# Third pair of tiles loaded before the token weights, with the first batch's work reordered and some evictions and casts moved to ScalarE

## The chip, the cores and the metric

One NeuronCore of a Trainium2 chip. The metric is the device time of one execution in microseconds (us). The profiled span of an execution is about 1.8 us shorter than its time.

## The reference

Two stages. The first is a linear recurrence per head with a decay, on q, k, v of shape 4 x 8 x 768 x 64. The second is a Wave-MLP on its result x (4 x 768 x 512).

```python
state = gamma * state + k_t v_t^T          # per batch and head
y_t   = scale * q_t state                  # x: heads side by side, 512 wide
theta = x @ w_theta
y     = w_tok_r @ (x * cos(theta)) + w_tok_i @ (x * sin(theta))   # over the 768 tokens
u     = x + y
out   = u + maximum(u @ w_ch, 0)
```

## The kernel before

The 768 tokens of a batch are three *pairs* of 128-token tiles, so there are twelve pairs. Pairs 0, 1, 2 are batch 0, and pair 3 opens batch 1. For each pair k, q and v are loaded (0.52 MB each), cast or scaled to bf16 ("prep"), k and q are flipped on TensorE, and the recurrence (called retention below) is done blockwise: attention block `ret_A`, mask on VectorE, product `ret_Y`, state products `ret_S` and `ret_I`. Then x is flipped back (`x_pe`), theta is made, ScalarE takes sine and cosine, and VectorE makes z (`zmul`). The token mixing `moe_M(m, lo, hi)` of output tile m takes z of tiles lo to hi. The token weights come as twelve tiles ("wtok", w0 to w5, real and imaginary), are cast and flipped (`w_cast`, `w_flip`, `w_out`). A flip is a transpose on TensorE, and an eviction is the copy of a result out of its PSUM bank, which frees the bank.

All loads are issued by one queue in program order, through buffers that are reused in turn:

```python
def load_wtok(r, t0):
    t = io.tile([P, S], FT, name="wtok", bufs=4)
    nc.sync.dma_start(out=t, in_=src[t0 * P:(t0 + 1) * P, :])
...
loads("p0 th p1 w0 p2 w1 w2 p3 w3 ch p4 w4 p5 w5")

def w_cast(t0):
    for r in range(2):
        row = work.tile([P, S], BF, name="wrow", bufs=5)
        nc.gpsimd.tensor_copy(row, wdma[r, t0])     # frees the wtok buffer
```

All transposes and the output products share two PSUM banks, tag "tr":

```python
ps   = psum.tile([P, 2, NP, P], BF, name="kq_ps", tag="tr", bufs=2)  # flip of k or q
w_ps = psum.tile([P, nT, P],    BF, name="w_ps",  tag="tr", bufs=2)  # flip of token weights
u_ps, o_ps, x_ps                                                     # the same two banks
```

The end of pair 3's iteration (n = nG = 3), cut:

```python
moe_M(first, 0, 2)                  # first = output tile 2
ret_S(n, 0); state_out(n, 0); ret_A(n, 1); ret_mask(n, 1); ret_Y(n, 0)
moe_U(done)                         # flips u of tiles 0 and 1
prep(n + 1, "k", (AC,)); preps(DP)  # q4: half on VectorE, half on GpSimd
moe_M(first, 2, 4)
w_tok(3)                            # flips w3, real and imaginary
moe_M(first, 4, nT); moe_u(first)
for i, t in enumerate(done):        # tiles 0 and 1
    flip(n + 1, "kq"[i])            # k4, then q4
    moe_O(t); moe_out(t)
```

Of the kernel before, what the change touches and what calls it, by code (L numbers as in the profile page):

```python
# [14 lines left out]
FT = mybir.dt.float32  # L15
BF = mybir.dt.bfloat16
# [16 lines left out]
def kernel(  # L33
# [17 lines left out]
    nc = tc.nc  # L51
# [39 lines left out]

    def load_wtok(r, t0):
        src = (moe_w_tok_r, moe_w_tok_i)[r]
        t = io.tile([P, S], FT, name="wtok", bufs=4)
        nc.sync.dma_start(out=t, in_=src[t0 * P:(t0 + 1) * P, :])
        wdma[r, t0] = t

    def loads(order):
        for what in order.split():
            if what == "th":  # L100
                load_w512("th", moe_w_theta)
            elif what == "ch":
                load_w512("ch", moe_w_ch)
            elif what[0] == "w":
                for r in range(2):
                    load_wtok(r, int(what[1:]))
            else:
                for name in "kqv":
                    load(int(what[1:]), name)

    loads("p0 th p1 w0 p2 w1 w2 p3 w3 ch p4 w4 p5 w5")


    warm = const.tile([P, dm], BF)
# [72 lines left out]
            copy(t, ps)  # L187
        st[n, name + "T"], st[n, name + "_ps"] = t, ps

    def flip_out(n, name):  # L190
        nc.vector.tensor_copy(st[n, name + "T"], st[n, name + "_ps"])

    def flip_dma(n, name):
        t = work.tile([P, 2, NP, P], BF, name="kqT", bufs=6)
# [109 lines left out]
    def x_out(n, copy):  # L304
        b, g = divmod(n, nG)
        copy(xs[b][:, 2 * g:2 * g + 2, :],
             st[n, "x_ps"].rearrange("p a j e -> p a (j e)"))

    def theta(n, a):
        th_ps = psum.tile([P, dm], FT, name="th_ps", tag="acc", bufs=2)  # L310
        for j in range(NP):
            nc.tensor.matmul(th_ps, st[n, "xT"][:, a, j, :], wth[:, j, :], start=(j == 0),  # L312
                             stop=(j == NP - 1))
        cs = work.tile([P, 2, dm], BF, name="cs", bufs=3)
        nc.scalar.activation(cs[:, 0, :], th_ps, AF.Sin, bias=halfpi, scale=1.0)  # L315
        nc.scalar.activation(cs[:, 1, :], th_ps, AF.Sin, bias=zerob, scale=1.0)  # L316
        st[n, "cs", a] = cs
# [53 lines left out]

    def moe_out(m):
        b, t0 = divmod(m, nT)
        ot = work.tile([P, dm], FT, name="ot", bufs=8)
        nc.vector.scalar_tensor_tensor(ot, mo[m]["o"], 0.0, mo[m]["u"], ALU.max, ALU.add)  # L375
        mo[m]["ot"] = ot

# [3 lines left out]

    wrow = {}

    def w_cast(t0):
        for r in range(2):
            row = work.tile([P, S], BF, name="wrow", bufs=5)
            nc.gpsimd.tensor_copy(row, wdma[r, t0])  # L387
            wrow[r, t0] = row

    def w_flip(r, t0, copy=True):  # L390
# [12 lines left out]
    def w_tok(t0):  # L403
        for r in range(2):
            w_flip(r, t0)
# [56 lines left out]
    def keep_busy(times):  # L462
        for _ in range(times):
            nc.tensor.matmul(warm_ps, warm[:, 0:P], warm, start=True, stop=True)
# [35 lines left out]
    theta(0, 1)  # L500
    flip(1, "q")
    prep(1, "v", PP)
    w_cast(0)
    x_pe(0, None)
    ret_A(1, 0)
    ret_mask(1, 0)
    x_out(0, DV.tensor_copy)
    keep_busy(3)
    ret_S(1, 0)
    state_out(1, 0)  # L510
# [1 line left out]
    ret_mask(1, 1)  # L512
    ret_Y(1, 0)
    ret_I(1, 0)
    w_flip(0, 0)
    ret_S(1, 1)
    state_out(1, 1)
    ret_I(1, 1)
    ret_Y(1, 1)
    ret_out(1, 0, AC.copy)  # L520
    ret_out(1, 1, DV.tensor_copy)
    w_flip(1, 0)
    prep(2, "k", (PL,))
    zmul(0, 0)
    flip(2, "k")
    prep(2, "q", DP)
    theta(1, 0)
    zmul(0, 1)
    theta(1, 1)
    moe_M(0, 0, 1)  # L530
    flip(2, "q")
    prep(2, "v", PP)
    w_cast(1)
    w_cast(2)
    x_pe(1, AC.copy)
    moe_M(0, 1, 2)
    ret_A(2, 0)
    ret_mask(2, 0)
    ret_S(2, 0)
    state_out(2, 0)  # L540
    ret_A(2, 1)
    ret_mask(2, 1)
    zmul(1, 0)
    ret_Y(2, 0)
    ret_I(2, 0)
    ret_I(2, 1)
    w_flip(0, 1, False)
    w_flip(1, 1, False)
    ret_Y(2, 1)
    ret_out(2, 0, AC.copy)  # L550
    ret_out(2, 1, DV.tensor_copy)
    w_out(0, 1)
    w_out(1, 1)
    zmul(1, 1)
    prep(3, "k", (PL,))
    moe_M(0, 2, 3)
    theta(2, 0)
    flip(3, "k")
    prep(3, "q", DP)
    theta(2, 1)  # L560
    moe_M(0, 3, 4)
    x_pe(2)
    w_flip(0, 2, False)
    w_out(0, 2, AC.copy)
    moe_M(1, 0, 2)
    zmul(2, 0)
    flip(3, "q")
    prep(3, "v", PP)
    w_cast(3)
    moe_M(1, 2, 4)  # L570
    zmul(2, 1)
    moe_M(0, 4, 5)


    tiles_of = {nG - 2: [], nG - 1: [0, 1]}
# [16 lines left out]
    for n in range(nG, B * nG + 1):  # L592
        mine, done = tiles_of[n], tiles_of[n - 1]
        late, two = n > nG, len(mine) > 1
        nxt = n + 1 in pairs

        if nxt and n + 1 >= K_DMA:
            flip_dma(n + 1, "k")
        if nxt and n + 1 >= Q_DMA:
            flip_dma(n + 1, "q")  # L600
        if n <= X_DMA and n + 3 in pairs:
            load(n + 3, "k")
        if n >= U_DMA:
            moe_U_dma(done[1])
        def preps(engines):
            prep(n + 1, "q", engines)
            prep(n + 1, "v", PP)
            if n in (nG, nG + 1):
                w_cast(n - nG + 4)

        if n == nG:
            nc.gpsimd.tensor_copy(wch, wdma["ch"])
        if nG + 3 < n + 1 < Q_DMA:
            preps(PP)
        if late:
            ret_I(n - 1, 1)

        if n in pairs:
            ret_A(n, 0)
            ret_mask(n, 0)  # L620
        if n == nG:
            moe_M(0, 5, nT)
            w_flip(1, 2)
            moe_u(0)
            moe_M(1, 4, nT)
            moe_u(1)
        if late:
            ret_Y(n - 1, 1)
            ret_S(n - 1, 1)
            ret_out(n - 1, 0, nc.scalar.copy)  # L630
            ret_out(n - 1, 1, nc.scalar.copy)
            state_out(n - 1, 1)
            if n < nG + 3:
                prep(n + 1, "k", (PL,))
                if n > nG + 1:
                    preps(DP)
            if n - 1 >= X_DMA:
                x_dma(n - 1)
        if n > X_DMA and n + 3 in pairs:
            load(n + 3, "k")  # L640
        if n + 3 in pairs:
            load(n + 3, "q")

        first = mine[0]
        moe_M(first, 0, 3 if two else 2)
        if late:
            theta(n - 1, 0)
            if n - 1 < X_DMA:
                x_pe(n - 1)
            if n == nG + 1:  # L650
                preps(DP)
            theta(n - 1, 1)
        if two:
            moe_M(first, 3, nT)
            moe_u(first)
        for name, limit in (("k", K_DMA), ("q", Q_DMA)):
            if nxt and nG + 1 < n + 1 < limit and (n > nG + 1 or name == "k"):
                flip(n + 1, name)
        if n + 1 >= K_DMA and not two:
            moe_M(first, 2, 4)  # L660
        if n + 3 in pairs:
            load(n + 3, "v")
        for t in stores_in(n):
            store(t)
        if n + 1 >= U_DMA:
            moe_U_dma(first)

        if n in pairs:
            ret_S(n, 0)
            state_out(n, 0)  # L670
            ret_A(n, 1)
            ret_mask(n, 1)
            ret_Y(n, 0)
            ret_I(n, 0)
        if n < U_DMA:
            moe_U(done)
        if n == nG:
            prep(n + 1, "k", (AC,))
            preps(DP)
        if n == nG or n + 1 < K_DMA and not two:  # L680
            moe_M(first, 2, 4)
        early_z = late and n < nG + 3
        if early_z and n > nG + 1:
            zmul(n - 1, 0)
        if n < nG + 3:
            w_tok(n - nG + 3)
        if early_z:
            zmul(n - 1, 0 if n == nG + 1 else 1)
        if not two:
            moe_M(first, 4, nT)  # L690
            if n == nG + 1:
                flip(n + 1, "q")
            moe_u(first)
            if n == nG + 1:
                zmul(n - 1, 1)
        elif n in pairs:
            moe_M(mine[1], 0, nT)
        if n + 2 in pairs and n > nG + 1:
            prep(n + 2, "k", (AC,))
        if n + 2 in pairs and n + 2 >= Q_DMA:  # L700
            prep(n + 2, "q", PP)
            prep(n + 2, "v", PP)
        if two and n in pairs:
            moe_u(mine[1])
        for i, t in enumerate(done):
            if n == nG:
                flip(n + 1, "kq"[i])
            moe_O(t)
            moe_out(t)
        if late and not early_z:  # L710
            zmul(n - 1, 0)
            zmul(n - 1, 1)
        if n not in pairs:
            moe_M(mine[1], 0, nT)
            moe_u(mine[1])
# [43 lines left out]
```

## Time and profile before

| | before |
|---|---|
| time, median | 168.45 us (167.87 to 168.82, 4 runs) |
| span of the profiled run | 166.5 us |
| TensorE / VectorE / ScalarE / GpSimd busy | 93 / 61 / 48 / 40 % |
| pair 3's first state product starts | 41.55 us |
| pair 4's iteration starts (state product `ret_I` of pair 3) | 48.41 us |

The chain of waits that ended last (this is its summary by engine) is almost all TensorE, so TensorE's own work sets the time, apart from the early waits.

```profile
PE 77%; DVE 12%; DMA 3%; issue 3%; ACT 1%; POOL 1%; DVEq 0%; SPq 0%; POOLq 0%
```

The load queue (SP) in the kernel before, around the token weights. The columns are start, length of the issue, queue and line, tile and source. w1's second tile, the two tiles of w2, and pair 3's k:

```profile
21.65 0.43 SPq L95 DMA_DIRECT2D wtok<-in_moe_w_tok_i_dram  x1
22.18 0.36 SPq L95 DMA_DIRECT2D wtok<-in_moe_w_tok_r_dram  x1
22.65 0.39 SPq L95 DMA_DIRECT2D wtok<-in_moe_w_tok_i_dram  x1
23.09 0.43 SPq L81 DMA_DIRECT2D pair<-in_k_dram  x1
```

### The profile page before, as it was taken

The numbers are of one execution on the slowest core, as the hardware profiler recorded it, in microseconds if no ns is written. First come the engines' busy times: TensorE is split into PE (matmuls) and PEld (weight loads), VectorE is DVE, ScalarE is ACT, GpSimd is POOL, SyncE is SP. The second block draws the span as 40 slices with busy tenths as digits, with TensorE's granted clock in tenths as the row PEclk, the third lists the DMA queues.
The fourth block names the chain that finished last, engine by engine and source line by source line (L and its number), as shares of the span: only waits on it lengthen the run. The fifth ranks groups of instructions, "written<-read, shape, count | busy, mean of one in ns | idle before, by whom it ended". The sixth has DMA issues, their size and how long they took to land.

```text
span 166.5 us, 4614 instructions
## 1 busy us (share of the span) xinstructions
PE 155.2 (93%) x1933; PEld 87.2 (52%) x1959; DVE 102.4 (61%) x137; ACT 79.1 (48%) x137; POOL 66.6 (40%) x82
## 2 busy tenths in 40 slices
PE   6969897899999999999999999999999999999991
PEld 2345664664755667555555554455545444444460
DVE  2257798878686699939446464584554736334442
ACT  7216568371819467687847827447083350000010
POOL 6275959786685877771442703600000000000000
PEclk9999999999999999999999999999999999999999
DMA  4999999999999999999999999998996161753343
GB/s 122 309 345 307 326 326 354 286 328 317 293 311 349 277 278 331 309 202 250 206 231 298 163 242 203 195 233 168 266 145 185 32 189 32 231 115 100 106 141 135
DMA packets 68901, 38.45 MB, mean 231 GB/s; under 512 B 26256, under 2 KB 63376, under 8 KB 68880
## 3 DMA queue, kind: packets, MB, share of 16 engines
q1 hardware_dynamic: 68736, 38.02, 90.2%
q8 instruction: 15, 0.25, 0.7%
q10 hardware_dynamic: 144, 0.13, 0.2%
q14 instruction: 6, 0.05, 0.1%
HBM read 25.69 MB, written 6.29 MB: 192 GB/s over the span
## 4 chain that ended last, share of the span: by engine, by line
PE 77%; DVE 12%; DMA 3%; issue 3%; ACT 1%; POOL 1%; DVEq 0%; SPq 0%; POOLq 0%
PE y_ps L340 33%; PE o_ps L368 12%; PE th_ps L312 11%; PE at_ps L208 4%; PE yT_ps L231 4%; DVE at L215 4%; DMA pair<-in_q_dram 3%; PE yT_ps L245 3%; PE st_ps L262 3%; PE kq_ps L183 3%; DVE z L322 2%; PE w_ps L393 2%; DVE kqT L187 2%; PE y_ps L420 2%; DVE kqb L175 1%
## 5 line engine op out<-in xcount | busy, mean ns | idle before, releaser
L340 PE MATMUL y_ps<-z,wtr 128*128 128x512 bf16 x133 | 50.5, 379 | 1.1
L340 PE MATMUL y_ps<-z,wti 128*128 128x512 bf16 x122 | 46.2, 379 | 0.4 <-issue 0.2
L347 DVE TENSOR_TENSOR u<-y_ps,x_sb 128x512 bf16<-128x512 f32 x23 | 15.9, 690 | 27.0 <-PE y_ps L340 27.0
L215 DVE TENSOR_TENSOR at<-at_ps,maskp 128x1024 bf16<-128x1024 f32 x24 | 29.3, 1221 | 4.6 <-PE at_ps L208 4.6
L175 POOL TENSOR_TENSOR kqb<-pair,qscp 128x512 bf16<-128x512 f32 x17 | 19.3, 1150 | 28.9 <-DMA pair<-in_q_dram 26.0
L175 POOL TENSOR_TENSOR kqb<-pair,vscp 128x512 bf16<-128x512 f32 x24 | 26.6, 1131 | 5.0 <-DMA pair<-in_v_dram 4.9
L285 ACT CAST xT<-yT_ps 128x512 bf16<-128x512 f32 x20 | 13.5, 739 | 30.0 <-PE yT_ps L231 29.9
L375 DVE SCALAR_TENSOR_TENSOR ot<-o_ps,u 128x512 f32<-128x512 f32 x23 | 15.9, 690 | 13.2 <-PE o_ps L368 13.2
L312 PE MATMUL th_ps<-wth,xT 128*128 128x512 bf16 x93 | 23.2, 379 | 0.5 <-ACT xT L285 0.3
L368 PE MATMUL o_ps<-wch,uT 128*128 128x512 bf16 x92 | 22.8, 379 | 0.3
L340 PEld LDWEIGHTS <-wtr 128*128 128x128 bf16 x138 | 13.5, 98 | 13.8
L276 ACT CAST stbd<-st_ps 64x256 bf16<-64x256 f32 x40 | 14.7, 368 | 12.5 <-PE st_ps L262 12.0
L340 PEld LDWEIGHTS <-wti 128*128 128x128 bf16 x138 | 13.5, 98 | 13.6 <-ACT wti L400 0.4
L315 ACT ACTIVATE cs<-th_ps,halfpi 128x512 bf16<-128x512 f32 x24 | 16.5, 689 | 7.0 <-PE th_ps L312 6.6
L322 DVE TENSOR_TENSOR z<-cs,x_sb 128x1024 bf16<-128x1024 bf16 x24 | 18.8, 808 | 0.1
L316 ACT ACTIVATE cs<-th_ps,zerob 128x512 bf16<-128x512 f32 x24 | 16.5, 687 | 0.0
L312 PEld LDWEIGHTS <-xT 128*128 128x128 bf16 x96 | 8.9, 98 | 11.0 <-ACT xT L285 1.0
L368 PEld LDWEIGHTS <-uT 128*128 128x128 bf16 x92 | 8.8, 98 | 10.5 <-issue 0.6
L208 PE MATMUL at_ps<-kqT 64*64 64x128 bf16 x384 | 10.6, 221 | 2.6 <-DVE at L215 1.8
L430 ACT COPY uT<-u_ps 128x384 bf16<-128x384 bf16 (+1 forms) x2 | 0.7, 372 | 25.5 <-PE u_ps L429 25.5
L187 DVE COPY kqT<-kq_ps 128x1024 bf16<-128x1024 bf16 x14 | 9.6, 688 | 4.2 <-PE kq_ps L183 4.1
L387 POOL CAST wrow<-wtok 128x768 bf16<-128x768 f32 x12 | 10.5, 902 | 0.3 <-DMA wtok<-in_moe_w_tok_i_dram 0.2
(61 smaller groups left out, 164.4 us busy)
## 6 DMA issues: line engine op xcount, KB each, us to landing
pair<-in_k_dram SPq DMA_DIRECT2D x12, 512.0 KB, 6.7
pair<-in_q_dram SPq DMA_DIRECT2D x12, 512.0 KB, 7.7
pair<-in_v_dram SPq DMA_DIRECT2D x12, 512.0 KB, 8.2
out_dram<-ot SPq DMA_DIRECT2D x23, 256.0 KB, 2.6
wtok<-in_moe_w_tok_r_dram SPq DMA_DIRECT2D x6, 384.0 KB, 6.4
wtok<-in_moe_w_tok_i_dram SPq DMA_DIRECT2D x6, 384.0 KB, 5.8
w<-in_moe_w_theta_dram SPq DMA_DIRECT2D x1, 1024.0 KB, 8.3
w<-in_moe_w_ch_dram SPq DMA_DIRECT2D x1, 1024.0 KB, 8.5
```

The source lines that it names most:

```text
L175: engines[two].tensor_mul(dst[:, two], src[:, two], _bcast_last(sc[:, 2 * g + two], D))
L208: nc.tensor.matmul(at_ps[half, par, j, :], kT[rows, two, j, half], qT[rows, :, j, half], start=(j == 0), stop=(j == NP - 1), skip_group_ch ...
L215: nc.vector.tensor_mul(at.rearrange("p a j t -> p (a j) t"), at_ps.rearrange("p a j t -> p (a j) t"), _bcast_mid(maskp[:, two].rearrange(" ...
L276: nc.scalar.copy(stbd[(c + 1) % 2][sl, :, sl], st_ps[b][sl])
L312: nc.tensor.matmul(th_ps, st[n, "xT"][:, a, j, :], wth[:, j, :], start=(j == 0), stop=(j == NP - 1))
L315: nc.scalar.activation(cs[:, 0, :], th_ps, AF.Sin, bias=halfpi, scale=1.0)
L316: nc.scalar.activation(cs[:, 1, :], th_ps, AF.Sin, bias=zerob, scale=1.0)
L322: nc.vector.tensor_mul(zs[b][:, c], st[n, "cs", a], _bcast_mid(xs[b][:, c, :], 2))
L340: nc.tensor.matmul(y_ps, wT[r][:, s0, t0 * P:(t0 + 1) * P], zs[b][:, s0, r, :], start=(s0 == 0 and r == 0), stop=(s0 == nT - 1 and r == 1))
L347: nc.vector.tensor_add(u, mo[m]["y"], xs[b][:, t0, :])
L368: nc.tensor.matmul(o_ps, mo[m]["uT"][:, j, :], wch[:, j, :], start=(j == 0), stop=(j == nD - 1))
L375: nc.vector.scalar_tensor_tensor(ot, mo[m]["o"], 0.0, mo[m]["u"], ALU.max, ALU.add)
```

## The change

The intent: pair 2's retention should not wait for its tiles, so they are loaded ahead of the token weights. Mixing of batch 0 starts later, but then runs in one piece. VectorE is relieved of three k evictions, GpSimd of w2's casts, and pair 2's two z are made earlier in VectorE's order.

```diff
-        t = io.tile([P, S], FT, name="wtok", bufs=4)
+        t = io.tile([P, S], FT, name="wtok", bufs=5)
-    loads("p0 th p1 w0 p2 w1 w2 p3 w3 ch p4 w4 p5 w5")
+    loads("p0 th p1 p2 w0 w1 w2 p3 ch w3 p4 w4 p5 w5")
...                                   # preamble, after pair 1's attention
-    w_cast(0)                         # right after pair 1's v
+    w_cast(0)                         # now after pair 2's v, on GpSimd
+    flip(2, "k", None); flip_out(2, "k", AC.copy)
+    theta_mm(1, 1, "y"); sines(1, 1)  # theta split, into another bank
...                                   # batch 0's mixing, now in one piece
+    moe_M(0, 0, 3)
+    w_flip(0, 1); w_flip(1, 1)
+    moe_M(0, 3, 4)
+    zmul(2, 0); zmul(2, 1)
+    flip(3, "k", None); flip_out(3, "k", AC.copy)
+    prep(3, "q", DP); prep(3, "v", PP)
+    w_cast(2, AC.copy)
+    moe_M(0, 4, nT)
+    moe_M(1, 0, 2)
+    flip(3, "q"); moe_u(0)
+    moe_M(1, 2, nT)
+    w_flip(0, 2); w_flip(1, 2); moe_u(1)
...                                   # end of pair 3's iteration
-        moe_M(first, 0, 3 if two else 2)
+        moe_M(first, 0, 3 if two or n == nG else 2)
-        if n < nG + 3:
+        if nG < n < nG + 3:
             w_tok(n - nG + 3)
         for i, t in enumerate(done):
-            if n == nG:
-                flip(n + 1, "kq"[i])
+            if n == nG and i == 1:
+                flip(n + 1, "k", nc.scalar.copy)
+                w_tok(n - nG + 3)
+                flip(n + 1, "q")
             moe_O(t); moe_out(t)
```

(Cut: buffers of cs 3 to 4 and of ot 8 to 7, one more filler matmul, pair 2's evictions.)

More of the change, by code (lines that the diff above doesn't have):

```diff
@@ L188, in flip, with flip_out @@
         st[n, name + "T"], st[n, name + "_ps"] = t, ps
-    def flip_out(n, name):
-        nc.vector.tensor_copy(st[n, name + "T"], st[n, name + "_ps"])
+    def flip_out(n, name, copy=nc.vector.tensor_copy):
+        copy(st[n, name + "T"], st[n, name + "_ps"])
     def flip_dma(n, name):
@@ L309, in theta, with theta_mm @@
     def theta(n, a):
-        th_ps = psum.tile([P, dm], FT, name="th_ps", tag="acc", bufs=2)
+        theta_mm(n, a)
+        sines(n, a)
+    def theta_mm(n, a, tag="acc"):
+        th_ps = psum.tile([P, dm], FT, name="th_ps" if tag == "acc" else "y_ps", tag=tag,
+                          bufs=2 if tag == "acc" else 1)
         for j in range(NP):
@@ L313, in theta, with sines @@
                              stop=(j == NP - 1))
-        cs = work.tile([P, 2, dm], BF, name="cs", bufs=3)
+        st[n, "th", a] = th_ps
+    def sines(n, a):
+        th_ps = st[n, "th", a]
+        cs = work.tile([P, 2, dm], BF, name="cs", bufs=4)
         nc.scalar.activation(cs[:, 0, :], th_ps, AF.Sin, bias=halfpi, scale=1.0)
@@ L373, in moe_out @@
         b, t0 = divmod(m, nT)
-        ot = work.tile([P, dm], FT, name="ot", bufs=8)
+        ot = work.tile([P, dm], FT, name="ot", bufs=7)
         nc.vector.scalar_tensor_tensor(ot, mo[m]["o"], 0.0, mo[m]["u"], ALU.max, ALU.add)
@@ L382, with w_cast @@
     wrow = {}
-    def w_cast(t0):
+    def w_cast(t0, copy=nc.gpsimd.tensor_copy):
         for r in range(2):
             row = work.tile([P, S], BF, name="wrow", bufs=5)
-            nc.gpsimd.tensor_copy(row, wdma[r, t0])
+            copy(row, wdma[r, t0])
             wrow[r, t0] = row
@@ L507 @@
     x_out(0, DV.tensor_copy)
+    prep(2, "k", (PL,))
     keep_busy(3)
@@ L514 @@
     ret_I(1, 0)
-    w_flip(0, 0)
     ret_S(1, 1)
@@ L518 @@
     ret_I(1, 1)
+    flip(2, "k", None)
+    prep(2, "q", DP)
     ret_Y(1, 1)
@@ L521 @@
     ret_out(1, 1, DV.tensor_copy)
-    w_flip(1, 0)
-    prep(2, "k", (PL,))
-    zmul(0, 0)
-    flip(2, "k")
-    prep(2, "q", DP)
-    theta(1, 0)
-    zmul(0, 1)
-    theta(1, 1)
-    moe_M(0, 0, 1)
+    flip_out(2, "k", AC.copy)
+    keep_busy(1)
     flip(2, "q")
     prep(2, "v", PP)
-    w_cast(1)
-    w_cast(2)
-    x_pe(1, AC.copy)
-    moe_M(0, 1, 2)
+    theta(1, 0)
     ret_A(2, 0)
     ret_mask(2, 0)
+    zmul(0, 0)
+    x_pe(1, None)
+    theta_mm(1, 1, "y")
     ret_S(2, 0)
     state_out(2, 0)
+    sines(1, 1)
+    w_cast(0)
     ret_A(2, 1)
     ret_mask(2, 1)
-    zmul(1, 0)
+    x_out(1, DV.tensor_copy)
     ret_Y(2, 0)
@@ L546 @@
     ret_I(2, 1)
-    w_flip(0, 1, False)
-    w_flip(1, 1, False)
+    w_flip(0, 0, False)
     ret_Y(2, 1)
-    ret_out(2, 0, AC.copy)
-    ret_out(2, 1, DV.tensor_copy)
-    w_out(0, 1)
-    w_out(1, 1)
+    ret_out(2, 0, DV.tensor_copy)
+    ret_out(2, 1, AC.copy)
+    w_out(0, 0)
+    w_flip(1, 0)
+    w_cast(1)
+    theta(2, 0)
+    zmul(0, 1)
+    theta(2, 1)
+    zmul(1, 0)
     zmul(1, 1)
+    x_pe(2)
     prep(3, "k", (PL,))
-    moe_M(0, 2, 3)
-    theta(2, 0)
-    flip(3, "k")
-    prep(3, "q", DP)
-    theta(2, 1)
-    moe_M(0, 3, 4)
-    x_pe(2)
-    w_flip(0, 2, False)
-    w_out(0, 2, AC.copy)
+    moe_M(0, 0, 3)
+    w_flip(0, 1)
+    w_flip(1, 1)
+    moe_M(0, 3, 4)
+    zmul(2, 0)
+    zmul(2, 1)
+    flip(3, "k", None)
+    flip_out(3, "k", AC.copy)
+    prep(3, "q", DP)
+    prep(3, "v", PP)
+    w_cast(2, AC.copy)
+    moe_M(0, 4, nT)
     moe_M(1, 0, 2)
-    zmul(2, 0)
     flip(3, "q")
-    prep(3, "v", PP)
-    w_cast(3)
-    moe_M(1, 2, 4)
-    zmul(2, 1)
-    moe_M(0, 4, 5)
+    moe_u(0)
+    moe_M(1, 2, nT)
+    w_flip(0, 2)
+    w_flip(1, 2)
+    moe_u(1)
     tiles_of = {nG - 2: [], nG - 1: [0, 1]}
@@ L612 @@
             nc.gpsimd.tensor_copy(wch, wdma["ch"])
+            w_cast(n - nG + 3)
         if nG + 3 < n + 1 < Q_DMA:
@@ L620 @@
             ret_mask(n, 0)
-        if n == nG:
-            moe_M(0, 5, nT)
-            w_flip(1, 2)
-            moe_u(0)
-            moe_M(1, 4, nT)
-            moe_u(1)
         if late:
@@ L674 @@
             ret_I(n, 0)
+        if n == nG:
+            preps(DP)
         if n < U_DMA:
@@ L678 @@
             prep(n + 1, "k", (AC,))
-            preps(DP)
-        if n == nG or n + 1 < K_DMA and not two:
+        elif n + 1 < K_DMA and not two:
             moe_M(first, 2, 4)
@@ L689 @@
         if not two:
-            moe_M(first, 4, nT)
+            moe_M(first, 3 if n == nG else 4, nT)
             if n == nG + 1:
@@ L705 @@
         for i, t in enumerate(done):
-            if n == nG:
-                flip(n + 1, "kq"[i])
+            if n == nG and i == 1:
+                flip(n + 1, "k", nc.scalar.copy)
+                w_tok(n - nG + 3)
+                flip(n + 1, "q")
             moe_O(t)
```

## The prediction

> **What bounds the kernel now.** I read the page first, then a table by stages, then the timelines of the engines from 12 to 49 us, because the diff touches only that stretch.
>
> ```profile
> PE   6969897899999999999999999999999999999991
> DMA  4999999999999999999999999998996161753343
> PEclk9999999999999999999999999999999999999999
> ```
>
> One digit is 4.16 us. TensorE (PE) is over 90% busy from the ninth slice on; its only thin slices are in the first 33 us. The DMA engines are full from the second slice to about 117 us. The granted clock is full throughout. So there are two bounds early on, TensorE's work and the arrival of data, and later TensorE's alone.
>
> ```profile
> 24.00:28.00 4.00, 3.87 (x58) 2.35 (x57) 3.48 (x5) 3.36 (x6) 3.58 (x4) 1.00 1.03 375
> 28.00:32.00 4.00, 2.63 (x72) 2.04 (x69) 3.48 (x4) 1.37 (x4) 3.41 (x5) 1.00 1.17 298
> 32.00:36.00 4.00, 3.85 (x35) 2.44 (x36) 3.04 (x6) 3.49 (x7) 2.91 (x4) 1.00 0.98 311
> 40.00:44.00 4.00, 3.84 (x72) 2.28 (x71) 2.44 (x3) 2.17 (x5) 1.90 (x1) 1.00 1.03 267
> ```
>
> This is busy time by stage: TensorE first, then its weight loads, VectorE, ScalarE, GpSimd, clock, DMA share, GB/s. The stage from 28 to 32 us is the worst: 1.37 us of TensorE is idle. Over all stages from 4 to 44 us the GB/s column averages 318, so in that time the queue delivers a fixed stream and only its order can be chosen.
>
> The timeline shows where that idle time is: pair 2's retention waits for its own VectorE mask.
>
> ```profile
> 27.60 0.45 PE L262 MATMUL st_ps<-kqb 64*64 64x64 bf16 x16
> 29.12 0.42 PE L208 MATMUL at_ps<-kqT 64*64 64x128 bf16 x16 [1.07 <-DVE at L215]
> 31.46 0.38 PE L340 MATMUL y_ps<-z,wtr 128*128 128x512 bf16 x1
> 32.15 1.04 PE L312 MATMUL th_ps<-wth,xT 128*128 128x512 bf16 x4 [0.32 <-ACT xT L285]
> ```
>
> The third pair's retention runs that late because its tiles arrive late: GpSimd takes them as they land. The fourth line below is VectorE waiting for the fifth pair's q.
>
> ```profile
> 21.86 1.04 POOL L171 CAST kqb<-pair 128x1024 bf16<-128x1024 f32 x1 [0.98 <-DMA pair<-in_k_dram]
> 23.67 1.04 POOL L175 TENSOR_TENSOR kqb<-pair,qscp 128x512 bf16<-128x512 f32 x1 [0.77 <-DMA pair<-in_q_dram]
> 25.14 2.49 POOL L175 TENSOR_TENSOR kqb<-pair,vscp 128x512 bf16<-128x512 f32 x2 [0.42 <-DMA pair<-in_v_dram]
> 44.09 0.69 DVE L175 TENSOR_TENSOR kqb<-pair,qscp 128x512 bf16<-128x512 f32 x1 [0.60 <-DMA pair<-in_q_dram]
> ```
>
> **What the Trainium skill says.** "TensorE: Matmul & The Clock Gate", section Back-to-back issue gap, gives N/2.4 + 2.5 ns for an isolated matmul, 216 ns at N = 512, and 131 ns sustained. The trace agrees with the first: matmuls of 512 columns start every 0.215 us (36.86, 37.08, 37.29, 37.51). I count work with 0.216. "Perfetto Trace Analysis", section Identifying the Most-Contended Engine, warns that matmul busy time is no good measure of headroom; here one matmul counts 379 ns while the next starts 215 ns after it, so I count starts, not busy time. "DMA: Bandwidth & Descriptors", section Where 436 GB/s comes from, puts the memory side of a core at about 358 GB/s; 318 measured is close enough that I expect no more bytes per us. "SBUF — State Buffer", section Who interferes with whom, says that a VectorE instruction with two SBUF inputs contends with GpSimd's reads; the trace agrees: z of one size takes 0.68 us alone (at 30.72) and 1.20 beside GpSimd (at 36.21).
>
> **The change part by part.** The order of instructions from the start of pair 4's iteration to the end is the same in both kernels on all five engines. In the kernel before that iteration starts at 48.41 us (the state product before pair 4's attention). So the whole effect is how much earlier it starts, and what later waits do with that.
>
> *Loads.* Pair 2 (three tiles of 0.52 MB) moves ahead of w0 (0.79 MB), which is 0.79/0.318 = 2.5 us: q2 lands near 21 rather than at 23.67 us. With v1 in by 16.9 and 1.65 us a tile, I put k2 at 18.5, q2 at 20.2, v2 at 21.8, and w0 at 23 and 24.3 (before: 19.0 and 20.05), 4.5 us later. ch comes 2.5 us earlier and w3 3.3 us later, and from pair 4 on everything has the same bytes ahead of it: q4 should land at 44.1 as before. The fifth wtok buffer pays for w0's later cast: the sixth tile waits for GpSimd's cast of the first, now at about 24.7 instead of being issued at 22.65 us. By then some three tiles are still queued (3 x 1.2 us), so I expect no hole.
>
> *Work moved.* Filler matmuls: one more, 0.22 us. Three evictions of k (0.69 on VectorE, 1.03 on ScalarE, from the rows of such copies) move to ScalarE, VectorE's 3 x 0.6 is freed; x of pair 1 (0.6) and one w eviction (0.55) come back to VectorE. Two casts (2 x 0.83 on GpSimd, on ScalarE an estimated 0.8 each from 1.04 for 1024 columns) leave GpSimd. No TensorE work is removed.
>
> *The walk.* I followed the new order by hand with the durations above, from the attention of pair 1 at 18.34 us, which is unmoved. Mask 1 ends at 21.8; the flip of k2 fits before it, q2 is scaled by 22.4 and flipped at 22.7 to 23.1; k2 reaches SBUF through ScalarE at 24.2, so pair 2's attention starts at 24.3 instead of 27.38 us, 3.1 us earlier. Its mask wait is now covered by the x transposes, the second theta and the state product (0.45 + 0.86 + 0.35 = 1.7 us against a mask of 1.23), so the 1.07 us wait goes. The last product of pair 2 waits about 0.3 us for its mask; w0's second flip waits a little for a bank. The token mixing starts only at about 31.6 (25.16 before), but then runs without gaps: 24 matmuls, 5.2 us, with four w flips and pair 3's flips. Pair 3's attention comes at 39.2, and its first state product at 41.1 instead of 41.55 us, with two more mixing matmuls (0.43) already behind it. That is 0.45 + 0.43 = 0.9 us of TensorE time gained.
>
> *The end of the stretch.* What remains until pair 4's iteration costs TensorE 0.30 + 0.35 + 0.22 for retention, 0.45 for u, 1.30 for six mixing matmuls, two times 0.86 for the outputs, two times 0.45 for k4 and q4, and 0.67 for w3: 5.9 us, so 47.0 us if nothing waits. But q4 lands at 44.09. After it VectorE scales q4 (0.6), adds u of tile 2 (0.6), writes the first output (0.6): 45.9. The first flip of w3 needs that output's bank: 46.3. Its eviction (0.55) frees the bank for q4's flip: 46.9 to 47.4. Meanwhile ScalarE's eviction of w3i (0.80) ends at 47.55 and frees the bank for the second output: 47.6 to 48.45. So the chain hung on q4 and two transpose banks ends where the iteration starts today, and most of the 0.9 us turns into waiting.
>
> *Sum.* TensorE can be ready 0.9 us less 0.5 us (waits of that stretch that exist today and that I can't remove) to 1.4 us earlier (48.41 - 47.0); the q4 chain allows 0.0. I take 0.6 us, because my chain assumes that the two banks strictly alternate and that q4 comes no earlier, and each evicting step may be 0.1 to 0.2 us shorter than I put it: 168.4 - 0.6 = 167.8 us.
>
> **The rivals.** (1) *Gain carried through.* If q4 lands earlier, or the chain is shorter than I think, the full 1.4 us stays, since after 48 us the timeline shows TensorE and VectorE both near full and q6, landing at 59.36, taken up by VectorE only at 61.50: about 167.0. Against it stands the wait of VectorE for q4. (2) *Nothing, the stream is the bound.* GpSimd waits for each pair's tiles up to pair 6 (61.26), so a TensorE that is early only waits later: 168.4. For it: the DMA row of nines; against: the chain of waits has no DMA on it after the first q. (3) *A new hole in the queue.* The sixth wtok tile blocks all later loads behind GpSimd's cast of w0; if v2 comes late or the scaling is slowed by VectorE (2.49 us seen in place of 2.04), the queue drains and pairs 3 and 4 shift by 1 to 2 us: 169.5. Against it: 3.6 us of queued tiles at that moment. (4) *VectorE as the bound from 28 to 35 us*: five z products of 0.68 us, three retained evictions and x stand in a row before the mixing can run; beside GpSimd each z can take 1.2, five times 0.5 = 2.6 us late at worst: 169. Against: GpSimd has few tiles to read between its w1 casts and k3 at 31.3, since the w2 casts went to ScalarE.
>
> **Range and chances.** The early stretch holds about 3.9 us of TensorE idle time in all from 14.8 to 48.4 us (33.6 us less an estimated 29.8 of work at 0.216 a large matmul, 0.45 for eight transposes, 0.3 to 0.4 for a retention group). Removing 2% (3.4 us) would take nearly all of it, with the stream unchanged: 4%. Losing 2% needs rival 3 and 4 together: 2%. Eight in ten I give to 166.5 to 168.9, from all of the gain and a little more to a small loss, with 0.5 us for the spread of the three runs (167.87 to 168.82).
>
> **What would show it.** In the changed trace: pair 2's first attention group near 24.3; no wait of about 1 us on a mask between 24 and 30; mixing from about 31.6 without gaps; pair 3's first state product near 41.1; q4's scaling on VectorE still at 44.1; then TensorE waits of some 0.2 to 0.8 us before the flips of w3 and q4 and the second output; the state product that opens pair 4's iteration at 47.8 or a little later. I am wrong if q4 arrives over 0.5 us away from 44.1, if the gain at 41 us is not there, or if the stretch after 48.4 us, 118.1 us long, changes its length by more than 0.3 us.

## The result, and the profile after

The changed kernel takes 171.15 us in the median (171.05 to 171.27, 4 runs) against 168.45: 2.70 us slower. The ratio is 1.0164, interval 1.0133 to 1.0194. (A ratio is the mean time of one kernel's runs over that of the other's in the same rounds, so not quite the ratio of the medians.) The predicted range, 166.5 to 168.9, misses it.

The page of the changed kernel: one digit is 4.23 us here. TensorE's row has a 7 in the ninth slice and a 6 in the twelfth (46.6 to 50.8 us), where the kernel before shows only nines from the ninth to the last but one, and the chain of waits, the last line, now contains 17% DMA.

```profile
PE   7879888979969999999999999999999999999990
...
DMA  4999998999999999999999999978967161743433
...
PE 68%; DMA 17%; DVE 5%; SPq 2%; POOL 2%; ACT 2%; issue 1%; DVEq 0%; POOLq 0%
```

The stages, in the columns of the prediction's table (TensorE, weight loads, VectorE, ScalarE, GpSimd, clock, DMA share, GB/s): from 24 to 28 us the DMA share is below 1 and 326 GB/s flow instead of 375, and from 44 to 48 us TensorE idles for 1.03 us.

```profile
24.00:28.00 4.00, 3.87 (x89) 2.39 (x88) 3.47 (x4) 2.37 (x6) 3.45 (x5) 1.00 0.90 326
...
44.00:48.00 4.00, 2.97 (x24) 1.46 (x22) 2.47 (x4) 3.10 (x4) 1.62 (x2) 1.00 1.03 317
```

The load queue of the changed kernel, the answer to the fence of before. The second tile of w2, the sixth token-weight tile, is issued at 26.55 us; the queue had been standing since 21.95, and pair 3's k behind it waits with it.

```profile
21.30 0.65 SPq L95 DMA_DIRECT2D wtok<-in_moe_w_tok_r_dram  x1
26.55 0.33 SPq L95 DMA_DIRECT2D wtok<-in_moe_w_tok_i_dram  x1
26.92 0.43 SPq L81 DMA_DIRECT2D pair<-in_k_dram  x1
```

What it stood for, in GpSimd's timeline: the buffer of w0's first tile is freed by its cast, which starts within 0.1 us of the tile's landing and ends at 26.52. Then pair 3's k arrives 1.7 us and pair 4's q 2.2 us later than before (32.97 against 31.30 and 46.38 against 44.20 in GpSimd's timeline).

```profile
25.70 0.82 POOL L396 CAST wrow<-wtok 128x768 bf16<-128x768 f32 x1 [0.38 <-DMA wtok<-in_moe_w_tok_r_dram]
...
32.97 1.04 POOL L171 CAST kqb<-pair 128x1024 bf16<-128x1024 f32 x1 [3.53 <-DMA pair<-in_k_dram]
...
46.38 1.55 POOL L175 TENSOR_TENSOR kqb<-pair,qscp 128x512 bf16<-128x512 f32 x1 [3.29 <-DMA pair<-in_q_dram]
```

TensorE's timeline: pair 2's attention is where it was meant to be, at 24.56; the mask wait of 1.07 us is gone. A wait for z of 0.89 us is new, pair 3's first state product comes at 42.86, the flip of w3 waits 1.31 us for an output to leave its bank, and pair 4's iteration starts at 50.86 (last line).

```profile
24.56 0.42 PE L208 MATMUL at_ps<-kqT 64*64 64x128 bf16 x16
...
36.31 0.38 PE L349 MATMUL y_ps<-z,wtr 128*128 128x512 bf16 x1 [0.89 <-DVE z L331]
...
42.86 0.38 PE L262 MATMUL st_ps<-kqb 64*64 64x64 bf16 x12
...
48.28 0.83 PE L402 MATMUL w_ps<-ident,wrow 128*128 128x128 bf16 x12 [1.31 <-DVE ot L384]
49.42 0.61 PE L183 MATMUL kq_ps<-ident,kqb 128*128 128x128 bf16 x8 [0.31 <-DVE wtr L409]
...
50.86 0.39 PE L245 MATMUL yT_ps<-kqT,stbd 128*128 128x128 bf16 x4
```

VectorE's timeline shows what stands behind these waits. The two z take 2.16 us together where 1.2 were counted, q3's scaling 1.52 where 0.6 were counted (GpSimd scales its half of q3 from 34.67 to 35.71, beside the z, and v3 from 36.07 to 38.61, beside VectorE's half of q3), and q4's scaling waits for the load.

```profile
34.10 2.16 DVE L331 TENSOR_TENSOR z<-cs,x_sb 128x1024 bf16<-128x1024 bf16 x2
36.18 1.52 DVE L175 TENSOR_TENSOR kqb<-pair,qscp 128x512 bf16<-128x512 f32 x1
...
46.34 0.69 DVE L175 TENSOR_TENSOR kqb<-pair,qscp 128x512 bf16<-128x512 f32 x1 [1.53 <-DMA pair<-in_q_dram]
```

The loss by sections:

| section | before | after | lost |
|---|---|---|---|
| to pair 3's first state product | 41.55 | 42.86 | 1.31, with two mixing matmuls (0.43) more done |
| from there to pair 4's iteration | 6.86 | 8.00 | 1.14, with these 0.43 fewer to do |
| from there to the end of the span | 118.1 | 118.4 | 0.3 |

Before the experiments I had three theories. A: the standing queue is the cause. B: the new order of the stream is itself slower. C: the new order of work at the end of pair 3's iteration is the cause.

### The profile page after: what moved, and what is told of

Same layout as the page of the kernel before. It is cut to its first block, busy times and chain, and to the rows that moved or that the text cites. A ratio compares the mean times of both kernels' runs of the same rounds, so it can differ in the third digit from the quotient of the medians.

```text
span 169.3 us, 4642 instructions
## 1 busy us (share of the span) xinstructions
PE 157.9 (93%) x1960; PEld 87.2 (51%) x1960; DVE 102.3 (60%) x136; ACT 82.1 (48%) x140; POOL 63.9 (38%) x80
## 4 chain that ended last, share of the span: by engine, by line
PE 68%; DMA 17%; DVE 5%; SPq 2%; POOL 2%; ACT 2%; issue 1%; DVEq 0%; POOLq 0%
PE y_ps L349 30%; PE o_ps L377 11%; PE th_ps L317 10%; DMA pair<-in_q_dram 9%; DMA wtok<-in_moe_w_tok_r_dram 4%; DMA pair<-in_k_dram 4%; PE at_ps L208 3%; PE yT_ps L231 3%; PE yT_ps L245 2%; PE st_ps L262 2%; SPq L81 2%; PE y_ps L429 2%; DVE at L215 1%; PE kq_ps L183 1%; DVE kqT L187 1%
## 5 line engine op out<-in xcount | busy, mean ns | idle before, releaser
L349 PE MATMUL y_ps<-z,wtr 128*128 128x512 bf16 x138 | 52.4, 380 | 0.9 <-DVE z L331 0.9
L349 PE MATMUL y_ps<-z,wti 128*128 128x512 bf16 x138 | 52.3, 379 | 0.2 <-ACT wti L409 0.2
L175 POOL TENSOR_TENSOR kqb<-pair,vscp 128x512 bf16<-128x512 f32 x24 | 25.9, 1100 | 3.8 <-DMA pair<-in_v_dram 3.8
L317 PE MATMUL th_ps<-wth,xT 128*128 128x512 bf16 x92 | 22.3, 379 | 0.2
L324 ACT ACTIVATE cs<-th_ps,halfpi 128x512 bf16<-128x512 f32 x23 | 15.8, 688 | 7.1 <-PE th_ps L317 6.6
L331 DVE TENSOR_TENSOR z<-cs,x_sb 128x1024 bf16<-128x1024 bf16 x24 | 18.5, 806 | 0.0
L325 ACT ACTIVATE cs<-th_ps,zerob 128x512 bf16<-128x512 f32 x23 | 15.8, 687 | 0.0
L473 PE MATMUL y_ps<-warm 128*128 128x512 bf16 x28 | 10.1, 489 | 1.3 <-DVE warm L115 1.3
L187 DVE COPY kqT<-kq_ps 128x1024 bf16<-128x1024 bf16 x11 | 7.5, 689 | 5.8 <-PE kq_ps L183 5.8
```

Source lines behind the costliest of these rows:

```text
L175: engines[two].tensor_mul(dst[:, two], src[:, two], _bcast_last(sc[:, 2 * g + two], D))
L317: nc.tensor.matmul(th_ps, st[n, "xT"][:, a, j, :], wth[:, j, :], start=(j == 0), stop=(j == NP - 1))
L324: nc.scalar.activation(cs[:, 0, :], th_ps, AF.Sin, bias=halfpi, scale=1.0)
L325: nc.scalar.activation(cs[:, 1, :], th_ps, AF.Sin, bias=zerob, scale=1.0)
L331: nc.vector.tensor_mul(zs[b][:, c], st[n, "cs", a], _bcast_mid(xs[b][:, c, :], 2))
L349: nc.tensor.matmul(y_ps, wT[r][:, s0, t0 * P:(t0 + 1) * P], zs[b][:, s0, r, :], start=(s0 == 0 and r == 0), stop=(s0 == nT - 1 and r == 1))
```

## The experiments

The times were taken beside runs of the kernel before, whose median was 168.57 us for e1 to e4 and 168.47 us for e5 to e8 and for e9 to e11. The kernel before varies there between 167.6 and 169.8, so differences below about 0.5 us are not read.

### e1: the wait taken out of the queue

```diff
-        t = io.tile([P, S], FT, name="wtok", bufs=5)
+        t = io.tile([P, S], FT, name="wtok", bufs=6)
-        row = work.tile([P, S], BF, name="wrow", bufs=5)
+        row = work.tile([P, S], BF, name="wrow", bufs=4)
```

> The changed kernel with six buffers for the token-weight tiles in place of five (and four for their casts in place of five, to make room), so that the sixth tile's load waits for no cast. Theory A, the load queue stood still from 21.95 to 26.55 us behind that one tile: the sixth tile is issued near 22 us, pair 3's k lands at 31.3 to 31.8 instead of 32.92, pair 4's q at 44.1 to 44.7 instead of 46.27, pair 4's iteration starts near 48.4 instead of 50.86, time 168.0 to 168.8. Rival B, the new order itself makes the early stream slower (pair tiles in a row move at 285 GB/s): q of pair 4 still lands after 45.5, time above 170. Rival C, the new order of work around w3 and the two banks is what costs: q lands near 44.1 but the iteration still starts after 50, time above 170.

Measured: 170.18 us (169.69 to 170.57), ratio 1.0074 (1.0018 to 1.0129). The queue no longer stands:

```profile
21.25 0.94 SPq L95 DMA_DIRECT2D wtok<-in_moe_w_tok_r_dram  x1
22.23 0.54 SPq L95 DMA_DIRECT2D wtok<-in_moe_w_tok_i_dram  x1
22.87 1.00 SPq L81 DMA_DIRECT2D pair<-in_k_dram  x1
```

Pair 4's q is there by 43.00, when GpSimd starts on it, 3.4 us earlier than in the changed kernel. Yet pair 4's iteration starts at 50.48, only 0.4 us earlier in the profiled runs. TensorE still waits for z, and between the state product and the iteration it now waits for banks, not for q4 (VectorE scales q4 at 44.90 without waiting):

```profile
36.49 0.38 PE L349 MATMUL y_ps<-z,wtr 128*128 128x512 bf16 x1 [0.86 <-DVE z L331]
...
47.41 0.49 PE L402 MATMUL w_ps<-ident,wrow 128*128 128x128 bf16 x6 [0.27 <-DVE ot L384]
48.24 0.49 PE L402 MATMUL w_ps<-ident,wrow 128*128 128x128 bf16 x6 [0.34 <-POOL wrow L396]
...
49.62 1.02 PE L377 MATMUL o_ps<-wch,uT 128*128 128x512 bf16 x4 [0.44 <-ACT wti L409]
```

(The profile names a cast of GpSimd for the 0.34 us. GpSimd was then casting w4, which that flip does not read; ScalarE's eviction of k4, which frees the bank, ended at 48.19, and e6 and e2 name it for the same wait.)

What follows: the standing queue is real, and removing it is worth about 1 us of the 2.7 in the medians (1.5 by the ratios, 1.0164 less 1.0074, whose intervals just miss each other). A's own figures, 48.4 for the iteration and 168.0 to 168.8, were missed. B falls: the new order, without the hold, delivers 327 GB/s between 14.6 and 43 us, where the changed kernel had 303 and the kernel before 320. C's figures came true: q4 early, the iteration after 50, the time above 170.

### e2: pair 3 loaded before w2

```diff
-    loads("p0 th p1 p2 w0 w1 w2 p3 ch w3 p4 w4 p5 w5")
+    loads("p0 th p1 p2 w0 w1 p3 w2 ch w3 p4 w4 p5 w5")
```

> The changed kernel with one change in the order of loads: pair 3 is loaded before w2 instead of after it, so the tile that must wait for a cast stands behind pair 3. Theory A: pair 3's tiles are issued from about 21 us on without a pause, the cast of w0 at 25.7 is over before w2's second tile is reached, no stall, pair 4's q lands at 44.1 to 44.7, time 167.5 to 168.8. Rival B (order itself, more pair tiles in a row, seven of 0.5 MB before any relief): q lands at 46 or later, time 170.5 to 172. Rival C: time above 170.

Measured: 170.58 us (170.32 to 171.38), ratio 1.0107. The rows of the queue follow each other without a gap, but pair 4's q lands at 45.2, between what A and B had expected, because the stream moved only 254 and 266 GB/s from 28 to 32 us; why is not settled. Pair 4's iteration starts at 50.49, the same as in e1 with q4 more than 2 us later. So with this end a q4 that comes by about 45 us does not set that start, and A alone is not enough.

### e3: the old order of loads under the new order of work

```diff
-    loads("p0 th p1 p2 w0 w1 w2 p3 ch w3 p4 w4 p5 w5")
+    loads("p0 th p1 w0 p2 w1 w2 p3 w3 ch p4 w4 p5 w5")
```

> The changed kernel with the order of loads of the kernel before (w0 before pair 2, w3 before ch), five buffers kept; the order of work stays the changed one. Theory A: GpSimd still casts w0 only after it has scaled pair 2's v, which now lands at 25.1, so the cast ends near 28 and the sixth tile waits until then, 1.5 us longer than in the changed kernel: pair 4's q at 47 to 48.5, time 171.5 to 173.5. Rival B (the order of the stream costs): this undoes it, q at 44.1 to 44.7, time 168 to 169.5. Rival C: time 170 to 171.5, with q at 44.1.

Measured: 173.06 us (172.69 to 173.23), ratio 1.0243. As A had it: w0 is there early, but its cast stands on GpSimd behind pair 2's v and starts at 27.35, so the sixth tile is issued at 28.20, and VectorE scales q4 at 47.53.

```profile
22.22 0.43 SPq L95 DMA_DIRECT2D wtok<-in_moe_w_tok_r_dram  x1
28.20 0.33 SPq L95 DMA_DIRECT2D wtok<-in_moe_w_tok_i_dram  x1
28.57 0.43 SPq L81 DMA_DIRECT2D pair<-in_k_dram  x1
```

The size of this result is not the queue's alone. TensorE waited 1.45 us for pair 2's k, and then the granted clock fell to half for about 3.4 us (the clock column, third from the right, is 0.50 from 24 to 26 us and 0.82 and 0.83 in the two stages beside it). At half speed these 3.4 us can have cost up to 1.7 us, an estimate. The mean clock of all four runs is 0.986 to 0.989, so it was not this run alone. B and C fall by q4, which both had expected at 44.1 to 44.7; the time alone would not tell C (170 to 171.5) from A.

```profile
22.00:24.00 2.00, 0.85 (x8) 0.69 (x8) 0.19 (x1) 0.23 (x1) 1.18 (x2) 0.82 1.19 274
24.00:26.00 2.00, 2.00 (x27) 1.45 (x27) 1.24 (x2) 1.29 (x2) 2.00 (x2) 0.50 0.97 371
```

### e4: the old end of pair 3's iteration, queue as changed

```diff
-        if nG < n < nG + 3:
+        if n < nG + 3:
             w_tok(n - nG + 3)
-            if n == nG and i == 1:
-                flip(n + 1, "k", nc.scalar.copy); w_tok(n - nG + 3); flip(n + 1, "q")
+            if n == nG:
+                flip(n + 1, "kq"[i])
```

> The changed kernel with the end of pair 3's iteration as before: w3 flipped ahead of the mixing matmuls and outputs, k4 and q4 flipped ahead of the two outputs, k4 evicted by VectorE. Theory A: q of pair 4 still lands at 46.3 and what hangs on it is about as long, so the iteration starts between 50 and 51 and the time is 170.3 to 171.5. Rival C (the new order around w3 and the banks costs 2.5 us): the iteration starts near 48.7, time 168.5 to 169.3.

Measured: 170.54 us (170.42 to 171.45), ratio 1.0114; pair 4's iteration at 51.07. The time is in A's range, but not for A's reason: q4 came early here, GpSimd took it up at 44.98 and VectorE scaled it at 45.65 without waiting for it. The iteration was late because the state product came only at 43.78 (TensorE waited 0.64 and 0.88 us for z), and the restoration was not complete either: w3's second flip followed the u flips with no mixing between and waited 0.77 us for their bank. It says that the new end is not the whole cause, no more.

### e5, e6, e7: two more parts, on top of the six buffers

After e1 I formed theory D: three separate losses, the queue's hold, the wait for z, and the bank waits of the new end. e5 is e1 with the end of pair 3's iteration exactly as before (e4's edit, and tile 2's mixing in two, two and two steps). e6 is e1 with this edit, which gives TensorE work while VectorE makes the last two z:

```diff
-    moe_M(0, 4, nT)
-    moe_M(1, 0, 2)
+    moe_M(1, 0, 4)
+    moe_M(0, 4, nT)
     flip(3, "q")
     moe_u(0)
-    moe_M(1, 2, nT)
+    moe_M(1, 4, nT)
```

e7 is both.

> Six token-weight buffers as in e1, and the end of pair 3's iteration exactly as in the kernel before (also its mixing matmuls of tile 2 in two, two and two steps, which e4 had not restored). Theory D, three separate losses: the queue's hold (about 1.0 us by e1), the z products that VectorE makes late beside GpSimd (about 0.9 us at pair 3's first state product: 43.03 in e1 against 41.55 before, less 0.43 of work more), and the bank waits of the new end (about 1.0: 7.45 us in e1 from that state product to pair 4's iteration against 6.86 before with 0.43 of work more). Then this restores the end: state product near 42.6, iteration near 49.4, time 168.9 to 169.6. Rival E, the end is late only because VectorE is late, whatever its order: iteration at 50.2 or later and time 169.9 to 170.4.

e5 measured: 169.65 us (169.33 to 170.41), ratio 1.0074; state product 42.56, iteration 49.57. The trace is near theory D; the time lies between D's range and E's.

> Six token-weight buffers, and four steps of tile 1's mixing moved ahead of tile 0's last two steps, so that TensorE has 1.7 us of work while VectorE makes the last two z; nothing else moves. Theory D: the wait of 0.86 us on z goes, pair 3's state product comes at 42.1 to 42.5 instead of 43.03, time 169.0 to 169.7. Rival F, VectorE is the bound of this stretch (its scaling of q3, 1.5 us beside GpSimd, follows the z products): the wait only moves to q3's flip or to the mask, state product at 42.8 or later, time 169.9 to 170.4.

e6 measured: 169.25 us (168.60 to 169.46), ratio 1.0041; state product 41.91, iteration 49.36. The wait for z is gone; what is left of VectorE's lateness is 0.31 us at q3's flip:

```profile
37.68 0.62 PE L183 MATMUL kq_ps<-ident,kqb 128*128 128x128 bf16 x8 [0.31 <-DVE kqb L175]
41.91 0.38 PE L262 MATMUL st_ps<-kqb 64*64 64x64 bf16 x12
```

> All three: six token-weight buffers, the old end, and tile 1's mixing ahead of the z wait. Theory D: the losses add up, iteration of pair 4 at 48.3 to 48.9, time 168.0 to 168.9, level with the kernel before or a little better. Rivals E and F: 169.3 to 170.2.

e7 measured: 169.54 us (168.57 to 170.79), ratio 1.0062; iteration 48.97.

| kernel | state product | pair 4's iteration | pair 6's iteration | median |
|---|---|---|---|---|
| before | 41.55 | 48.41 | 68.83 | 168.45 |
| changed | 42.86 | 50.86 | 71.12 | 171.15 |
| e1, six buffers | 43.03 | 50.48 | 71.19 | 170.18 |
| e5, and old end | 42.56 | 49.57 | 69.62 | 169.65 |
| e6, and z covered | 41.91 | 49.36 | 69.69 | 169.25 |
| e7, all three | 41.38 | 48.97 | 69.68 | 169.54 |

Up to pair 4's iteration D holds in part in the profiled runs: e5 takes off 0.9 us, e6 1.1, both together 1.5 and not 2.0. In e7 q4 binds again: VectorE waits 1.17 us for it and scales it at 44.64, and the iteration starts 4.33 us later, just as in the kernel before (44.09 and 48.41, 4.32 us). A TensorE that is ready earlier gains nothing there. In the times, e6 is 0.9 us below e1; e5 is 0.5 below in the median and equal in the ratio, so the old end is worth something in the trace and is not resolved in the time. And e7 does not keep its lead: by pair 6's iteration it is level with e5 and e6. Its expectation, 168.0 to 168.9, was missed. In e7's trace TensorE waits 0.64 us there for VectorE: its scaling of q6 takes 1.38 us beside GpSimd, and the next flip waits for the eviction of x behind it.

```profile
62.58 1.38 DVE L175 TENSOR_TENSOR kqb<-pair,qscp 128x512 bf16<-128x512 f32 x1
63.88 0.68 DVE L306 COPY x_sb<-x_ps 128x1024 bf16<-128x1024 bf16 x1
```

### e8: z covered, queue as changed

The edit of e6 on the changed kernel, with its five buffers.

> The changed kernel with tile 1's mixing moved ahead of the z wait and nothing else: the queue's hold stays. Theory D with the queue as the outer bound: q of pair 4 lands at 45.0 to 46.3 and everything after it hangs on it, so TensorE's earlier arrival is lost, time 170.7 to 171.3. Rival G, the losses simply add whatever the queue does: 170.0 to 170.5.

Measured: 170.38 us (170.00 to 172.24), ratio 1.0129 (1.0078 to 1.0179). In the median this is 0.8 us below the changed kernel, so it falls in rival G's range, and the expected 170.7 to 171.3 was missed. The profiled run happens to be the slow one, 172.24. It shows TensorE waiting 1.90 us at w3's flip for a q4 that came at 46.0, and then the granted clock at half for about 3.4 us:

```profile
47.96 0.83 PE L402 MATMUL w_ps<-ident,wrow 128*128 128x128 bf16 x12 [1.90 <-DVE ot L384]
```

The same run by stages:

```profile
50.00:52.00 2.00, 2.00 (x10) 0.86 (x7) 0.84 (x2) 0.00 (x0) 1.22 (x3) 0.50 0.94 265
```

The other five runs have no trace. Their mean clocks are 0.995 to 1.000 against 0.983 here, so what they did at that place stays open.

### e9, e10, e11: q of pairs 5 and 6 scaled wholly by GpSimd

```diff
-                preps(DP)      # q: half on VectorE, half on GpSimd
+                preps(PP)      # for n = 4 and n = 5
```

on the kernel before (e9), on e7 (e10) and on e6 (e11).

> The kernel before with one edit: the scaling of q for pairs 5 and 6 done wholly by GpSimd (two halves of 1.04 us) instead of half by VectorE. GpSimd waits for the next tile of v anyway (1.54 and 0.51 us at 53.77 and 61.26), and VectorE loses an instruction of 0.68 and one of 1.35 us. Theory K, VectorE beside GpSimd is the outer bound between pair 4's and pair 6's iterations (20.42 us in the kernel before, VectorE busy 4.0 of 4 us from 60 to 68): those 20.4 us shrink to 19.2 to 19.9 and the time to 167.2 to 168.0. Rival L, it is the arrival of pair 6's tiles: no change within 0.3 us.

e9 measured: 168.21 us (167.52 to 169.27), ratio 0.9998 (0.9955 to 1.0040): no change, as rival L had it. From pair 4's to pair 6's iteration it took 20.12 us instead of 20.42. In this profiled run VectorE scaled q4 at 44.83 and pair 4's iteration started at 49.15, 0.74 us later than in the run of before, though nothing ahead of it differs: so much the stream alone varies from run to run. From q4's scaling to the iteration it is again 4.32 us.

> e7 (six buffers, old end, mixing ahead of the z wait) with the same edit of the scaling of q. Theory K: e7 reached pair 4's iteration at 48.97 and lost its lead over e5 and e6 by pair 6's iteration (69.68 against 69.62 and 69.69) to VectorE; with the edit the lead stays, pair 6's iteration at 68.4 to 69.0, time 168.0 to 168.8. Rival L: pair 6's iteration again at 69.4 to 69.8, time as e7, 169.2 to 169.8.

e10 measured: 168.76 us (168.23 to 169.56), ratio 1.0018 (0.9982 to 1.0054). Pair 4's iteration at 48.86, pair 6's at 68.84: 19.98 us in place of e7's 20.71, within theory K's range. Right afterwards it lost 0.77 us in the profiled run, where TensorE waited 0.70 us for a transpose by DMA of pair 7's k (7.15 us from 76.60 to 83.75 between two state products, 6.38 in the changed kernel).

> e6 (six buffers, mixing ahead of the z wait, the changed end) with the same edit. Theory K: pair 4's iteration at 49.4 as in e6, pair 6's 0.5 to 1.2 us earlier than its 69.69, time 168.0 to 168.8. Rival L: as e6, 169.0 to 169.5.

e11 measured: 169.22 us (169.00 to 169.29), ratio 1.0049; pair 4's iteration at 49.62, pair 6's at 69.63. The stretch is 0.3 us shorter than in e6 and the time is the same: rival L. The stretch is 0.3 to 0.7 us shorter with the edit than in the kernel it was made on, in all three. But that is no evidence for K: without the edit the same stretch took 19.97 us in e2, 19.98 in e4 and 20.05 in e5, as short as with it (19.98 to 20.12), so the runs differ by as much on their own. In the time only e10 lies more than 0.5 us below its kernel, 0.8 in the medians, and the intervals of the two ratios overlap. No kernel beats the kernel before clear of the noise; e9 and e10 are level with it.

## Why the prediction was wrong

**What held.** Pair 2's attention came at 24.56 (24.3 predicted). The mask wait of 1.07 us went. Mixing started at 31.79 (31.6). The stretch from pair 4's iteration to the end kept its length, 118.4 against 118.1 us. The statement that the whole effect is the start of pair 4's iteration was right: it accounts for 2.45 of the 2.8 us between the two spans. That the rest kept its length so closely is in part luck: from pair 4's to pair 6's iteration, where the order is the same in the kernel before, the changed kernel and e1 to e8, the profiled runs took 19.97 to 20.71 us.

**The step that failed first: "By then some three tiles are still queued (3 x 1.2 us), so I expect no hole."** The wait of the sixth tile was seen, and rival 3 named it, with 169.5 us, but its cost was mis-sized. I had w0's cast at about 24.7; it started at 25.70 and ended at 26.52, and the tile was issued at 26.55. Three tiles were indeed still under way: GpSimd took up w0's second and w1's two from 26.69 on, and w2's first came after them. What the step left out is the time from issue to landing. The sixth tile landed 4.6 us after its issue, the shortest such time of a token-weight tile in that run, and even in e3, where nothing was left ahead of it, it took 3.1. So 3.6 us of queued tiles could not cover it: from 26 to 28 us the stream fell to 267 GB/s (260 in e4 and 234 in e8, where the queue also stood until about 26.1) against 382 in e1. GpSimd took up pair 3's k at 32.48 to 32.97 in these three runs, and at 31.07 to 31.82 in five of the six runs with six buffers (32.83 in e11), and "q4 should land at 44.1 as before" became 46.3 (44.9 in e4, 45.9 in e8). e1 shows that the hold costs about 1 us of time.

The times from issue to landing of the token-weight tiles, from the profile's view of that tile, in the changed kernel and in e3:

```profile
DMA to landing us min/median/max: 4.6/7.3/7.9
...
DMA to landing us min/median/max: 3.1/6.1/7.9
```

That the cast itself came late has another part. k2, q2 and v2 were taken up at 19.97, 21.77 and 23.28 where I had them landing at 18.5, 20.2 and 21.8. The 1.65 us a tile was not the error, since they follow each other by 1.80 and 1.51; all of the 1.5 us lies between v1, taken up at 16.79, and k2, 3.2 us later. Then w0's first tile came 2.4 us after v2 instead of 1.2. The stream moved less than my 318 GB/s there (285 from 16 to 20 us, 254 from 20 to 22); why these two gaps are so long is not shown.

**The second: the walk to the state product at 41.1.** It came at 42.86, and at 43.03 even in e1 where the queue did not stand. The walk gave each z 0.6 us in place; the last two took 2.16, and q3's scaling 1.52 for 0.6. This was rival 4's mechanism, put at five z products and dismissed because GpSimd has few tiles to read there; three of the z did run in 1.88 us together, but the last two met GpSimd's scaling of q3 and v3. Covering the wait (e6) brought the state product to 41.91; the 0.8 us that are left hold 0.31 at q3's flip and were not broken down further.

**The third: the end of the stretch.** I computed 7.35 us from state product to pair 4's iteration by the q4 chain (41.1 to 48.45), then discounted it by 0.6 us with the argument that steps may be shorter. Nothing in the trace supported this. The chain itself was right: from q4's scaling to the iteration I had 4.36 us (44.09 to 48.45), and it took 4.52 (46.34 to 50.86). The discount was the error. The whole section took 8.00 us, and 7.45 or 7.46 in e1, e2, e6 and e11, where q4 is earlier: the chain through the two banks (output, w3's flip, its eviction, q4's flip, second output) is long by itself. In e5 and e10 the old order makes it 7.01 with 0.43 us more work inside. Of the 1.57 us lost in this section (1.14, and the 0.43 of work that it no longer holds) q4's lateness is then about 0.55 (8.00 less 7.45) and the rest mostly the banks. One slip of the text changes nothing: 33.6 less 29.8 us is 3.8, not 3.9.

**What stays open.** e1's gain is 0.4 us of span in the profiled runs, 1.0 in the medians and 1.5 by the ratios; single profiled runs of one order differ by 0.7 us, so the shares above are no finer than that. Why e7's lead is lost by pair 6 was seen in one trace (VectorE beside GpSimd), and e9 to e11 don't settle it. Why e2's stream is slow from 28 to 32 us is open.

## What to carry to other kernels

When loads are issued by one queue in order, the length of a buffer ring decides which load may stop all others: for each reordering, write down for every load which instruction frees its buffer, when that instruction can run at the earliest, and what is queued behind it. Compare such a wait not only with what is still queued: the load that waited needs its own time from issue to landing (4.6 us here) before anything can use it. And when TensorE is given an earlier start, look for the engine that feeds it, because here VectorE and two transpose banks took back what the earlier load had gained.

## What the Trainium skill lacked or had wrong

- "TensorE: Matmul & The Clock Gate", section Back-to-back issue gap: it gives about 131 ns as the sustained spacing of matmuls of 512 columns. No stretch here shows it; back-to-back matmuls of that size start every 0.215 us and never closer, which is the figure that this section gives for an isolated one. (Elsewhere the page has about 216 ns for back-to-back ones too; it is this section that does not fit.)
- The same page, section "HAM oscillation — how this bites in real kernels": it puts the re-throttling at idle gaps above about 3.4 us. Here a single TensorE wait of 1.45 us (e3) and one of 1.90 us (e8) were each followed by 3.4 us at a granted clock of 0.50; a wait of 1.31 us (the changed kernel) was not.
- "DMA: Bandwidth & Descriptors", section Where 436 GB/s comes from: it says that for transfers from memory the side of about 358 GB/s binds, and doesn't repeat there what the page says just before, that this is a core's share when both cores of a memory stream. The prediction took it as a limit; this core alone went past it: 385 GB/s from 24 to 26 us in the kernel before, 408 from 36 to 38 us in e2.
- None of the pages I read spells out what follows for a ring of buffers, that one load waiting for its buffer stops every later load of the same issuing queue. Here it stood from 21.95 to 26.55 us, and removing the wait was worth about 1 us of time.
- "SBUF — State Buffer", section Who interferes with whom, names the contention of VectorE and GpSimd without a size for this kind of instruction: in the changed kernel three z products took 1.88 us together while GpSimd was idle, and two took 2.16 us beside it. Both engines can lose: VectorE's half of q3 took 1.52 us at 36.18, where GpSimd's scaling of v3 had begun at 36.07; its half of q4 took 0.69 us at 46.34, and GpSimd's half, begun at 46.38, took 1.55 instead of 1.04.
